# Attention, then a two-layer ELU network, on one core: where v is cast, how reciprocals are spread, and who turns q and k to fp16

## The chip, the cores and the metric

One NeuronCore of a Trainium2 chip runs the whole program in one launch. The time is device time in microseconds (us), from the runs of the program; beside it stands the span of one profiled execution, from its first to its last instruction. Lower is better.

## The reference

```python
B, H, S, D = 8, 8, 576, 64                     # q, k, v: fp32
q_d, k_d, v_d = means of q, k, v over groups of 4 tokens      # 144 tokens
out_d  = softmax(q_d @ k_d.T / 8) @ v_d                       # "global"
scores = where(|i - j| < 4, q @ k.T / 8, -1e9)
local  = softmax(scores) @ v                                  # "local"
x = (repeat(out_d, 4) + local)      # -> 4608 tokens x 512
h = x @ w_in                        # 512 x 2048
g = where(h > 0, h, exp(min(h, 0)) - 1)
out = g @ w_out                     # 2048 x 512, fp32
```

## The kernel before

**Work.** Attention is done by pairs of heads: eight batches b of four pairs j. Local attention runs in six blocks of 96 queries against 102 keys (three more on either side), so v is held as 102 rows. The network is done by nine tiles t of 512 tokens: `mm1(t, fc)` (L561) makes 128 columns of h from four matmuls, takes them through ScalarE (exp, L572) and VectorE (L573, L576); `mm2(t, i)` (L580) is a quarter of an output row block, again four matmuls, and with every fourth ScalarE copies the result (L593) and SyncE stores it (L595).

**One pair.** `early_transposes` (b below 3, L250) or `transposes` (b from 3, L307) turn q and k on TensorE, by products with constants. `flip` (L241, matmul at L244) does it in two halves: head e uses 64 columns of the array and writes 64 partitions. The same step makes the means of v (L273 or L314). ScalarE and VectorE copy the results to `qt`, `kt`, `kd`, `vd`. A memset by VectorE clears the six edge columns of each new `kt` (L259, L327). `scores` (L339) has the products (L346, L361), the exponentials (L369, L375) and the mask (L380). Row sums are made for a batch at a time by `denominators` (L421), with the reciprocal at L448; these 128 x 288 numbers must then be spread over the partitions of the heads. For batch 1 `spread_pe` (L470) does it by matmuls and copies; for batches 2 to 7 `spread_out` and `spread_in` (L451, L456) write them to DRAM and read them back, both from ScalarE's queue. `outputs` (L546) has the last products (L506, L512), two VectorE multiplications (L521, L526) and GpSimd's addition into `xt` (L535), the network's input. Batch 0 has versions of its own, pair by pair (`early_v`, `early_denominators`, `early_spread`, `early_outputs`).

**Loads.** q and k come by half batches n (four heads) through `load_qk` (L194) on GpSimd's queue, which casts to fp16 on the way. v comes by half batches as fp32 through `load_v` (L215) on SyncE's queue: 96 rows, then three rows above and three below. `open_v` (L224) takes the buffers and has GpSimd clear a few elements first, for which SyncE waits. `cast` (L236) turns one pair's v to fp16 on GpSimd. Weights come in eight chunks by `load_weights` (L166) on GpSimd's queue, cast on the way.

**Order.** The schedule is written out by hand. All calls are put in one list of events with a time each and sorted (L663); each engine and each queue works in that order. A unit is about one mm1 and one mm2. The startup is the list `order` with `after`; the network's tile t starts at `start_of(t)`; batch b from 1 on starts at `base` with its pairs at `slots`, its row sums at `d0` and its outputs at `o0`. In `order`, all q and k of batch 0, both halves of v and four weight chunks are issued before the first cast of v. Results of the transposes, scores, outputs and spreads share two PSUM buffers (`two`, L131), so each waits for the copies out of the one before the last.

Of the kernel before, what the change touches and what calls it, by code (L numbers as in the profile page):

```python
# [19 lines left out]
QW = QB + 24  # L20
# [9 lines left out]
NHALF = 2 * B  # L30
# [70 lines left out]
def kernel(  # L101
# [76 lines left out]
    stq, stk, stv, stv32 = {}, {}, {}, {}  # L178
    stT, stB, stS, stR = {}, {}, {}, {}

    def heads(b, j):

        n, a = 2 * b + j // 2, 2 * (j % 2)
        return stq[n], stk[n], stv[n], a

    def blocks(src, n, lo, hi, tok, rows_):

        a = src[n // 2, 4 * (n % 2)]
        return bass.AP(
            tensor=a.tensor, offset=a.offset + (QB * lo + tok) * D,  # L190
            ap=[[D, rows_], [QB * D, hi - lo], [1, D]],
        )

    def load_qk(n, pairs_=(0, 1)):  # L194
        if n not in stq:
            stq[n] = sb.tile([QB, 4, NB, 64], FP16, tag="q16", bufs=3, name="q16")
            stk[n] = sb.tile([QB, 4, NB, 64], FP16, tag="k16", bufs=3, name="k16")
        h0, h1 = 2 * pairs_[0], 2 * pairs_[-1] + 2
        for src, dst in ((q, stq[n]), (k, stk[n])):
            if n < 2 * NRUN:  # L200
                a = src[n // 2, 4 * (n % 2) + h0]
                nc.gpsimd.dma_start(
                    out=dst[:, h0:h1].rearrange("p h c d -> p h (c d)"),
                    in_=bass.AP(
                        tensor=a.tensor, offset=a.offset,
                        ap=[[NB * D, QB], [S * D, h1 - h0], [1, NB * D]],
                    ),
                )
            else:
                nc.gpsimd.dma_start(  # L210
                    out=dst[:].rearrange("p h c d -> p (h c) d"),
                    in_=blocks(src, n, 0, 4 * NB, 0, QB),
                )

    def load_v(n):  # L215
        v32 = stv32[n]
        lo = 1 if n == 0 else 0
        hi = 4 * NB - (1 if n == NHALF - 1 else 0)
        to = v32[:].rearrange("p h c d -> p (h c) d")
        nc.sync.dma_start(out=to[3:99], in_=blocks(v, n, 0, 4 * NB, 0, QB))  # L220
        nc.sync.dma_start(out=to[0:3, lo:], in_=blocks(v, n, lo, 4 * NB, -3, 3))
        nc.sync.dma_start(out=to[99:KW, 0:hi], in_=blocks(v, n, 0, hi, QB, 3))

    def open_v(n):  # L224

        v32 = sb.tile([KW, 4, NB, 64], FP32, tag="v32", bufs=2, name="v32")
        if n == 0:
            nc.gpsimd.memset(v32[0:3, 0, 0, :], 0.0)
        if n == NHALF - 1:
            nc.gpsimd.memset(v32[96:KW, 3, NB - 1, :], 0.0)  # L230
        if n < 2 * NRUN:
            nc.gpsimd.memset(v32[:, 0, 0, 0:1], 0.0)
        stv32[n] = v32
        stv[n] = sb.tile([KW, 4, NB, 64], FP16, tag="v16", bufs=4, name="v16")

    def cast(b, j):  # L236
        n, a = 2 * b + j // 2, 2 * (j % 2)
        nc.gpsimd.tensor_copy(out=stv[n][:, a : a + 2], in_=stv32[n][:, a : a + 2])  # L238
# [11 lines left out]
    def early_transposes(b, j):  # L250
        q16, k16, v16, a = heads(b, j)
# [5 lines left out]
        kt = sb.tile([128, S + 6], FP16, tag="kt", bufs=2, name="kt")  # L257
        kd = sb.tile([128, SD], FP16, tag="kd", bufs=2, name="kd")
        nc.vector.memset(_free(kt[:, 0:1], [[S + 3, 2], [1, 3]]), 0.0)  # L259
        tq, tk = two("tq"), two("tk")  # L260
        for t, x16 in ((tq, q16), (tk, k16)):
# [8 lines left out]
            if b >= NEARLY:  # L270
                g = 0 if t is tq else 1
                for c in range(3):
                    nc.tensor.matmul(  # L273
                        t[0:KG, 0, HB : HB + 128], VR[:, 48 - 24 * c : 120 - 24 * c],
                        v16[:, a : a + 2, 3 * g + c, :], start=(c == 0), stop=(c == 2),
# [14 lines left out]
    def early_v(b, j):  # L290

        mex, dex, _ = stS[(b, j)]
        _, _, v16, a = heads(b, j)
        rb = early_two("rb")
        VR = consts["VR"]
        for c in range(NB):
            nc.tensor.matmul(  # L297
                rb[0:KG, c // 3, 360:488], VR[:, 48 - 24 * (c % 3) : 120 - 24 * (c % 3)],
                v16[:, a : a + 2, c, :], start=(c % 3 == 0), stop=(c % 3 == 2),
# [7 lines left out]
    def transposes(b, j):  # L307
        q16, k16, v16, a = heads(b, j)
        VR, QI = consts["VR"], consts["QI"]
        tq, tk = two("tq"), two("tk")  # L310
        for c in range(NB):
            flip(tq, q16, a, c, (c // 3, QW * (c % 3)), QW, QI, start=True, stop=True)
        for c in range(NB):
            nc.tensor.matmul(  # L314
                tq[0:KG, c // 3, 3 * QW : 3 * QW + 128],
                VR[:, 48 - 24 * (c % 3) : 120 - 24 * (c % 3)], v16[:, a : a + 2, c, :],
# [6 lines left out]
        for c in range(NB):  # L323
            flip(tk, k16, a, c, (c // 3, QW * (c % 3)), QW, QI, start=True, stop=True)
        tk4 = tk[:, :, 0 : 3 * QW].rearrange("p g (c w) -> p g c w", w=QW)
        kt = sb.tile([128, S + 6], FP16, tag="kt", bufs=2, name="kt")
        nc.vector.memset(_free(kt[:, 0:1], [[S + 3, 2], [1, 3]]), 0.0)  # L327
# [173 lines left out]
    def output_products(b, j, lg):  # L501
        mex, dex, vd = stS.pop((b, j))
        _, _, v16, a = heads(b, j)
        for c in range(NB):
            for e in range(2):
                nc.tensor.matmul(  # L506
                    lg[64 * e : 64 * e + 64, c // 3, QB * (c % 3) : QB * (c % 3) + QB],
                    v16[:, a + e, c, :], mex[:, e, QB * c : QB * c + QB], start=True, stop=True,
# [93 lines left out]
    def at(time, fn, *args):  # L602
# [5 lines left out]
        (load_consts, 0, 3), (load_qk, 0, (0,)), (load_qk, 0, (1,)), (open_v, 0), (load_v, 0),  # L608
        (load_qk, 1), (open_v, 1), (load_v, 1),
        *((load_weights, i) for i in range(4)), (cast, 0, 0), (cast, 0, 1),  # L610
        (warm, 9), (early_transposes, 0, 0), (warm, 5), (scores, 0, 0), (load_consts, 3, 4),
        (warm, 5), (load_weights, 4), (load_weights, 5), (cast, 0, 2), (cast, 0, 3),
        (load_weights, 6), (load_weights, 7),
    ]
    after = {2: ((open_v, 2), (load_v, 2), (load_qk, 2)),
             3: ((load_qk, 3), (open_v, 3), (load_v, 3))}
# [11 lines left out]
    def start_of(t):  # L628
        return 0 if t == 0 else 16 * t + (16 if t == 1 else 20)
# [66 lines left out]
```

## Time and profile before

| | |
|---|---|
| runs, median of 3 (least, most) | 417.18 us (414.22, 418.7) |
| the profiled execution's own time | 414.35 us |
| its span | 412.6 us |
| mean granted TensorE clock | 0.953 |
| busy: TensorE, VectorE, ScalarE, GpSimd | 372.1, 253.1, 202.0, 107.4 us |
| first matmul on v of batch 0 (L297) | at 25.41 us |
| first mm1 (L567) | at 46.13 us |
| first transposes of batch 1 | at 58.50 us |
| two blocks of four 512-column matmuls, start to start | 0.87 us |
| VectorE, min with -1 added (L573), mean of 144 | 0.371 us |

How to read it: PE is TensorE, PEld its loads of weights, DVE VectorE, ACT ScalarE, POOL GpSimd, SP SyncE; a q behind a name is that engine's queue, where it issues a DMA. L238 is line 238 of the code. Busy time of PE is taken from modelled ends, so what counts for it is the time from one start to the next. In a line of the timeline stand the start and the length in us, the engine, the line, the operation, the result, what it reads, the shapes, how many were merged, and in brackets the idle time before it with what ended it.

### The profile page before, as it was taken

How to read it: one execution, taken by the hardware profiler on the slowest of the kernel's cores; microseconds unless marked ns; L12 is line 12 of the kernel's file. 1: busy time of each engine (PE TensorE's matmuls, PEld its weight loads, DVE VectorE, ACT ScalarE, POOL GpSimd, SP SyncE). 2: the span in 40 equal slices, each digit the busy share in tenths (PEclk: the TensorE clock that was granted, in tenths of full speed). 3: DMA queues.
4: the chain of work that ended last, by engine and by line, in shares of the span. 5: the costliest groups of instructions: out<-in, count | busy, mean ns of one | idle time of the engine just before them, and what ended most of it. 6: DMA issues, size and time to landing. Idle time of an engine off the chain costs nothing.

```text
span 412.6 us, 9302 instructions
## 1 busy us (share of the span) xinstructions
PE 372.1 (90%) x3847; PEld 191.6 (46%) x3847; DVE 253.1 (61%) x520; ACT 202.0 (49%) x381; POOL 107.4 (26%) x150
## 2 busy tenths in 40 slices
PE   8057898978986899999989999999999899999996
PEld 4045344545543455554545554545545354444442
DVE  2127497465863866686758676866867585555520
ACT  3025256624654466647554756475656334444421
POOL 7025543007430372072307130820230050000000
PEclk9759698999995799999999999999999999999999
DMA  8996979222997099709980999092200401010111
GB/s 142 215 188 100 187 130 193 55 55 36 180 130 115 2 116 96 159 27 149 92 154 29 168 82 169 21 151 53 81 27 25 106 27 51 25 52 26 52 52 76
DMA packets 107993, 39.16 MB, mean 95 GB/s; under 512 B 90540, under 2 KB 103214, under 8 KB 107950
## 3 DMA queue, kind: packets, MB, share of 16 engines
q0 software_dynamic: 55456, 13.63, 34.9%
q1 hardware_dynamic: 44698, 19.47, 21.4%
q10 hardware_dynamic: 7796, 5.46, 5.7%
q8 instruction: 30, 0.49, 0.5%
q14 instruction: 13, 0.11, 0.1%
HBM read 42.30 MB, written 9.88 MB: 126 GB/s over the span
## 4 chain that ended last, share of the span: by engine, by line
PE 72%; DVE 10%; DMA 6%; ACT 5%; ACTq 3%; issue 2%; SPq 1%; POOL 1%; DVEq 0%; POOLq 0%
PE op L587 27%; PE hp L567 26%; DMA v<-in_v_dram 4%; PE sc L346 4%; DVE gt L576 3%; PE tq L244 3%; PE tk L244 3%; ACTq L461 3%; PE lg L506 2%; DMA rd<-rc 2%; PE tq L314 2%; DVE e L573 2%; DVE rc L448 1%; ACT pex L369 1%; ACT e L572 1%
## 5 line engine op out<-in xcount | busy, mean ns | idle before, releaser
L567 PE MATMUL hp<-xt,WI 128*128 128x512 f16 x576 | 151.8, 391 | 7.7 <-DVE gt L576 6.2
L587 PE MATMUL op<-WO,gt 128*128 128x512 f16 x576 | 145.4, 380 | 0.0
L572 ACT ACTIVATE e<-hp 128x512 f16<-128x512 f32 x144 | 85.7, 599 | 102.3 <-PE hp L567 81.5
L576 DVE SCALAR_TENSOR_TENSOR gt<-hp,e 128x512 f16<-128x512 f32 x144 | 99.6, 691 | 5.3
L567 PEld LDWEIGHTS <-WI 128*128 128x128 f16 x576 | 54.7, 100 | 75.3 <-issue 15.9
L573 DVE TENSOR_SCALAR e<-e 128x512 f16<-128x512 f16 x144 | 53.5, 371 | 57.7 <-ACT e L572 56.5
L535 POOL TENSOR_TENSOR xt<-ln,gn 128x512 f16<-128x512 f16 (+7 forms) x64 | 42.6, 694 | 157.7 <-DVE ln L526 157.6
L587 PEld LDWEIGHTS <-gt 128*128 128x128 f16 x576 | 53.5, 98 | 62.8 <-issue 0.5
L369 ACT ACTIVATE pex<-sc 102x576 f16<-102x576 f32 x64 | 41.4, 646 | 36.7 <-PE sc L361 36.4
L238 POOL CAST v<-v 102x768 f16<-102x768 f32 x32 | 26.1, 831 | 67.0 <-DMA v<-in_v_dram 56.9
L380 DVE TENSOR_TENSOR mex<-pex,const 102x1152 f16<-102x1152 f16 x28 | 21.7, 776 | 26.4 <-ACT pex L369 26.0
L593 ACT COPY os<-op 128x512 f32<-128x512 f32 x36 | 21.2, 588 | 17.9 <-PE op L587 17.9
L375 ACT ACTIVATE dex<-sc 72x288 f16<-72x288 f32 x64 | 25.8, 403 | 0.0
L346 PE MATMUL sc<-qt,kt 64*102 64x96 f16 x384 | 18.9, 221 | 4.8 <-DVE kt L284 2.8
L346 PEld LDWEIGHTS <-kt 64*102 64x102 f16 x384 | 13.5, 129 | 19.6 <-ACT e L572 6.3
L244 PEld LDWEIGHTS <-q 96*64 96x64 f16 x528 | 14.5, 111 | 15.7 <-issue 14.3
L244 PE MATMUL tq<-const,q 96*64 96x96 f16 (+1 forms) x528 | 19.0, 215 | 2.3 <-DVE ln L526 1.3
L526 DVE TENSOR_TENSOR ln<-lg,rcb 128x576 f16<-128x576 f32 x28 | 20.9, 746 | 0.0
L320 ACT CAST qt<-tq 128x720 f16<-128x720 f32 x20 | 15.1, 757 | 10.0 <-PE tq L314 10.0
L328 ACT CAST kt<-tk 128x576 f16<-128x576 f32 x20 | 12.8, 641 | 14.3 <-DVE kt L327 12.0
L244 PE MATMUL tk<-const,k 96*64 96x96 f16 (+1 forms) x528 | 18.9, 215 | 0.1
L297 PE MATMUL rb<-v,const 102*72 102x128 f16 x24 | 2.4, 244 | 15.6 <-POOL v L238 14.4
(67 smaller groups left out, 269.1 us busy)
## 6 DMA issues: line engine op xcount, KB each, us to landing
v<-in_v_dram SPq DMA_DIRECT2D x16, 576.0 KB
out_dram<-os SPq DMA_DIRECT2D x36, 256.0 KB
q<-in_q_dram POOLq DMA_DIRECT2D x15, 288.0 KB, 7.5
k<-in_k_dram POOLq DMA_DIRECT2D x15, 288.0 KB, 8.9
rcb<-rd ACTq DMA_DIRECT2D x12, 288.0 KB
WI<-in_moe_w_in_dram POOLq DMA_DIRECT2D x4, 512.0 KB, 17.0
WO<-in_moe_w_out_dram POOLq DMA_DIRECT2D x4, 512.0 KB, 7.6
rcb<-rd ACTq DMA_DIRECT2D x12, 72.0 KB
```

The lines of the kernel that those rows point to most:

```text
L238: nc.gpsimd.tensor_copy(out=stv[n][:, a : a + 2], in_=stv32[n][:, a : a + 2])
L244: nc.tensor.matmul(t[64 * e : 64 * e + 64, col[0], col[1] : col[1] + w] if len(col) == 2 else col[2](t[64 * e : 64 * e + 64, 1, col[1] : c ...
L346: nc.tensor.matmul(sc[e][0:KW, c // 3, QB * (c % 3) : QB * (c % 3) + QB], kt[r, QB * c : QB * c + KW], qt[r, QB * c : QB * c + QB] if run ...
L369: nc.scalar.activation(out=pex[:, e, :].rearrange("p (g u) -> p g u", g=2), in_=sc[e][0:KW, :, 0:HB], func=AF.Exp, scale=SCALE,)
L375: nc.scalar.activation(out=dex[:, e], in_=sc[e][0:KG, :, HB : HB + SD], func=AF.Exp, scale=SCALE,)
L380: nc.vector.tensor_tensor(out=mex[:], in0=pex[:], in1=mk2, op=AB.mult)
L535: nc.gpsimd.tensor_tensor(out=xt(t)[:, j, t0 - TBLK * t : t1 - TBLK * t], in0=ln[:, a:z], in1=_rep4(gn[:, a // 4 : z // 4]), op=AB.add,)
L567: nc.tensor.matmul(hp[:], WI[:, dc, 128 * fc : 128 * fc + 128], x[:, dc, :], start=(dc == 0), stop=(dc == DMC - 1),)
L572: nc.scalar.activation(out=e[:], in_=hp[:], func=AF.Exp)
L573: nc.vector.tensor_scalar(out=e[:], in0=e[:], scalar1=1.0, scalar2=-1.0, op0=AB.min, op1=AB.add)
L576: nc.vector.scalar_tensor_tensor(out=gts[t][:, fc, :], in0=hp[:], scalar=0.0, op0=AB.max, in1=e[:], op1=AB.add)
L587: nc.tensor.matmul(op_[:], gts[t][:, fc, 128 * tt : 128 * tt + 128], WO[:, fc, :], start=(fc == 0), stop=(fc == FCN - 1),)
```

## The change

**v and its cast.** v is loaded pair by pair (`load`), three SyncE loads each, into buffers of one pair (three of them). In the startup the first pair's v is issued after the first pair's q and k; weight chunk 0 comes after the cast of pair 0, chunk 1 after that of pair 2, chunks 2 and 3 after that of pair 3, chunks 4 to 7 after the outputs of pairs 0 and 1. v as fp16 is laid out by block, then head.

**Reciprocals.** Batch 2, too, is spread by `spread_pe`.

**Batches 3 to 7.** q and k are loaded pair by pair as fp32 on SyncE's queue, and `cast` turns q, k and v to fp16 on GpSimd, with the two heads of a block side by side. `transposes` then flips both heads with one matmul over the whole array.

**Beside these.** `kt` has two fixed buffers, cleared once. Batch 1 starts at 15.5 instead of 11.5, with closer pairs; tiles from 1 on start 3 units later; mm2 of tile 0 comes every 1.35 units instead of 1.5; batch 2's outputs come 1.5 to 1.7 units sooner after its start.

```diff
+    kts = [sb.tile([128, S + 6], FP16, tag=f"kt{i}", bufs=1, name=f"kt{i}") for i in range(2)]
+    for t in kts:
+        nc.vector.memset(_free(t[:, 0:1], [[S + 3, 2], [1, 3]]), 0.0)
...
+    def load(b, j):
...
+        ts = []
+        if b >= NRUN:
+            for src, name in ((q, "q32"), (k, "k32")):
+                t = sb.tile([QB, 2, NB, 64], FP32, tag=name, bufs=3, name=name)
+                nc.sync.dma_start(out=flat(t), in_=rows(src, 0, 2 * NB, 0, QB))
+                ts.append(t)
+        v32 = sb.tile([KW, 2, NB, 64], FP32, tag="v32", bufs=3, name="v32")
+        lo, hi = 0, 2 * NB
+        if (b, j) == (0, 0):
+            lo = 1
+            nc.gpsimd.memset(v32[0:3, 0, 0, :], 0.0)
+            nc.gpsimd.memset(v32[:, 0, 1, 0:1], 0.0)
...
+        nc.sync.dma_start(out=to[3:99], in_=rows(v, 0, 2 * NB, 0, QB))
+        nc.sync.dma_start(out=to[0:3, lo:], in_=rows(v, lo, 2 * NB, -3, 3))
+        nc.sync.dma_start(out=to[99:KW, 0:hi], in_=rows(v, 0, hi, QB, 3))
+        st32[(b, j)] = (*ts, v32)
+
     def cast(b, j):
-        n, a = 2 * b + j // 2, 2 * (j % 2)
-        nc.gpsimd.tensor_copy(out=stv[n][:, a : a + 2], in_=stv32[n][:, a : a + 2])
+        st16[(b, j)] = []
+        for t, name in zip(st32.pop((b, j)), ("q16", "k16", "v16") if b >= NRUN else ("v16",)):
+            p = t.shape[0]
+            if name == "v16":
+                x = sb.tile([p, NB, 2, 64], FP16, tag=name, bufs=8, name=name)
+            else:
+                x = sb.tile([p, 2, NB, 2, 64], FP16, tag=name, bufs=3, name=name)[:, 0]
+            nc.gpsimd.tensor_copy(
+                out=x if name != "v16" else x[:], in_=t[:].rearrange("p e c d -> p c e d")
+            )
+            st16[(b, j)].append(x)
...
     def transposes(b, j):
...
         for c in range(NB):
-            flip(tq, q16, a, c, (c // 3, QW * (c % 3)), QW, QI, start=True, stop=True)
+            nc.tensor.matmul(
+                tq[:, c // 3, QW * (c % 3) : QW * (c % 3) + QW], q16[:, c], QI, start=True, stop=True
+            )
...
     order = [
-        (load_consts, 0, 3), (load_qk, 0, (0,)), (load_qk, 0, (1,)), (open_v, 0), (load_v, 0),
-        (load_qk, 1), (open_v, 1), (load_v, 1),
-        *((load_weights, i) for i in range(4)), (cast, 0, 0), (cast, 0, 1),
-        (warm, 9), (early_transposes, 0, 0), (warm, 5), (scores, 0, 0), (load_consts, 3, 4),
-        (warm, 5), (load_weights, 4), (load_weights, 5), (cast, 0, 2), (cast, 0, 3),
-        (load_weights, 6), (load_weights, 7),
+        (load_consts, 0, 3), (load_qk, 0, (0,)), (load, 0, 0), (load_qk, 0, (1,)), (load_qk, 1),
+        (load, 0, 1), (load, 0, 2), (cast, 0, 0), (load_weights, 0), (load, 0, 3), (cast, 0, 1),
+        (load, 1, 0), (warm, 9), (early_transposes, 0, 0), (warm, 5), (scores, 0, 0),
+        (load_consts, 3, 4), (warm, 5), (cast, 0, 2), (load, 1, 1), (load_weights, 1), (cast, 0, 3),
+        (load, 1, 2), (load_weights, 2), (load_weights, 3),
     ]
-    after = {2: ((open_v, 2), (load_v, 2), (load_qk, 2)),
-             3: ((load_qk, 3), (open_v, 3), (load_v, 3))}
+    after = {0: ((load_weights, 4), (load_weights, 5)), 1: ((load_weights, 6), (load_weights, 7)),
+             2: ((load_qk, 2),), 3: ((load_qk, 3),)}
...
-        return 0 if t == 0 else 16 * t + (16 if t == 1 else 20)
+        return 0 if t == 0 else 16 * t + (19 if t == 1 else 23)
...
-            base, slots, d0, o0 = 11.5, (0, 1.4, 3.1, 4.5, 6.2, 7.6, 9.3, 10.7), 12.0, (17.2, 18.4)
+            base, slots, d0, o0 = 15.5, (0, 1.4, 2.8, 4.2, 5.6, 7.0, 8.4, 9.8), 12.0, (17.2, 18.4)
...
-            base, slots, d0, o0 = start_of(b) - 24, TIGHT, 12.8, (20.4, 22)
+            base, slots, d0, o0 = start_of(b) - 24, TIGHT, 12.8, (18.9, 20.3)
...
-            n = 2 * b + j // 2
+            n = NPAIR * b + j + 3
             at(base + (slots[2 * j - 2] if j else -3.1) + 0.1, cast, b, j)
+            if n < len(pairs):
+                at(base + slots[2 * j] + 0.2, load, *pairs[n])
+            if b + 1 < NRUN and j % 2:
+                at(base + slots[2 * j] + 0.3, load_qk, 2 * b + 2 + j // 2)
...
-        if b == 1:
+        if b < NRUN:
             at(base + d0 + 2.4, spread_pe, b, 0)
             at(base + d0 + 3.3, spread_pe, b, 2)
...
-            at(16 + 1.5 * s + 0.75 if t == 0 else start_of(t + 1) + s + 0.75, mm2, t, s)
+            at(16 + 1.35 * s + 0.75 if t == 0 else start_of(t + 1) + s + 0.75, mm2, t, s)
```

## The prediction

> **What bounds the kernel now.** I read the busy slices first, for where TensorE (PE) is short of work; then the waits and the chain, for what it waits for; then the timeline of those places; last one stretch where PE is full.
>
> ```profile
> PE   8057898978986899999989999999999899999996
> PEclk9759698999995799999999999999999999999999
> ```
>
> A slice is 10.3 us. There are two holes: near 11 to 25 us, and around 120 to 135 us, each with a lowered clock. From slice 14 on PE is full. So the first 145 us are bounded by waits and the rest by PE's own instructions.
>
> ```profile
> PE rb L297 <- POOL v L238: 14.4, 1, 14.4
> POOL v L238 <- DMA v<-in_v_dram: 56.9, 8, 16.0
> ```
> ```profile
> 8.48 15.90 DMA v<-in_v_dram
> ```
>
> The waits (us in total, times, longest) and the chain agree: PE stands 14.4 us for the cast of the first v, and that for a load of v that ends at 24.38. The packets in the trace say why: v's begin at 6.0 us and run at about 400 per us until 10, then, once the 1024-byte packets of the weights run beside them, at 55 to 160 per us.
>
> ```profile
> 119.08 1.95 DVE L448 RECIPROCAL rc<-den 128x288 f16<-128x288 f32 x1
> ...
> 127.86 2.65 ACTq L461 DMA_DIRECT2D rcb<-rd  x4
> 130.55 0.60 ACT L572 ACTIVATE e<-hp 128x512 f16<-128x512 f32 x1 [4.75 <-issue]
> 132.25 1.87 PE L567 MATMUL hp<-xt,WI 128*128 128x512 f16 x4 [3.08 <-DVE gt L576]
> ```
>
> The second hole (timeline: start, us, instruction): batch 2's reciprocals go through DRAM, ScalarE (ACT) stands 4.75 us in that, the first mm1's exponentials stand behind it, and PE waits 3.08 us.
>
> ```profile
> 165.81 0.51 PE L244 MATMUL tq<-const,q 96*64 96x120 f16 x12
> 166.24 0.53 PE L314 MATMUL tq<-v,const 102*72 102x128 f16 x6
> 166.70 0.51 PE L244 MATMUL tk<-const,k 96*64 96x120 f16 x12
> 167.14 1.04 PE L587 MATMUL op<-WO,gt 128*128 128x512 f16 x4
> 168.01 1.03 PE L567 MATMUL hp<-xt,WI 128*128 128x512 f16 x4
> ```
>
> PE in the full part: 0.87 us from one block of four 512-column matmuls to the next, 0.44 us for 12 half-array flips. (T(b,j) below: the transposes of pair j of batch b; block: four matmuls of mm1 or mm2.)
>
> **The change part by part.** The profiled execution took 414.35 us (span 412.6); the runs' median, 417.18, is 2.8 above it. The sum is against 414.35.
>
> *1. Startup.* v comes by pairs, three SyncE (SP) loads each; v(0,0) goes ahead of most of q and k, and its memset now stands behind two of POOL's DMA issues (1.31 to 2.73), not four, so SP issues at about 3.2, packets from 4.9 (1.7 us later, as in the trace). It needs 1152 packets and two small ones instead of 2304. Beside it run the 1190 or so q/k packets left, at 145 per us (6 to 12 us): 8.2 us, so v(0,0) lands at about 13.5. Bounds: 8 us at 390 packets per us (then PE's own end of T(0,1) at 11.4 counts) and 24.4 as now. I take 13.5, with rows for both queues behind it. Cast 0.83: PE resumes at about 15, not 25.4. Batch 0 then takes the 20.7 us of 25.41 to 46.13: mm1 begins at 35.7. POOL's weight issues (0.76 each) now wait for casts: chunk 0 at 15, chunk 1 at 19, 2 and 3 at about 24, the rest behind batch 0's sums of xt, which wait for DVE's ln. At 155 packets per us (16 to 24 us) the 4096 weight packets and at 190 batch 1's 768 first q/k packets take 30.5 us from about 17, with 2 us of gap: 50. mm1 of tile 0, now all 16 blocks before T(1,0), takes 16 x 0.9 and 1.7 for the low clock: 51.8. So T(1,0) stands at 51.8 against 58.50, with 16 blocks done instead of 12 (3.5 us): **-10.2**, bounds 0 and -13.
>
> *2. Batch 1.* T(1,0) to T(1,2) took 13.5 us (58.50 to 72.04) with five blocks between. With mm2 alone between, T(1,2) to T(1,3) took 4.82 (72.04 to 76.86), so 9.6 with four blocks: 3.9 less, less one block of 0.87: **-3.0**. Into batch 2 mm1 stands one block closer to the xt that it needs (0.9), and each of four pairs has a block fewer around it (0.5 each): **+3**. Bounds of both: -5 and +5, the idle around the same steps now.
>
> *3. Batch 2's reciprocals by PE.* Added, by batch 1's rows: 12 matmuls (0.48 and 0.67 us), four casts each on ACT and DVE (0.64 and 0.28; 0.76 and 0.30, twice). Removed: five ACT DMAs (0.33, 2.65) and the 4.75 us. New waits: both PSUM pairs are held by the scores' exponentials (2.1 us on ACT) when the first spread comes, with no block between; the second and the next transposes wait for casts (0.55 and 1.05); the outputs come right after scores (2.0). Queued behind each on PE are the blocks of mm1. From the end of den I get 22.5 us to T(3,2), where now 25.4 go by (118.15 to 143.58); DVE is then nearly full: **-2** after taking out the part of step 4 in it. Bounds: +3 if the clock falls twice, -5 if it never does (it is 0.5 from 124.7 to 138.3).
>
> *4. Whole-array flips, batches 3 to 7.* Starts of the single matmuls: two halves go side by side every 53 ns, so six whole flips of 120 columns cost no less than twelve halves: 0.32 us. What goes is the switching. From flips to L314 it is 146 ns instead of 53, L314 to flips 149 instead of 56, block to flips 309 instead of 216, flips to block 148 instead of 53; within each run the first step is 74 instead of 53. Between 128*128 forms, and from 102*72 (L273) to 128*128, there is no such gap (55 to 56 ns). 93+93+93+95+21+21 = 416 ns a pair; two of the 20 pairs are in step 3: 18 x 0.416 = **-7.5**. Bounds 0 (the 96-row weights switch too) and -8.3. I take the full gain: L412's whole-array matmuls follow each other every 42 ns.
>
> The Trainium skill (TensorE: Matmul & The Clock Gate, Part 3) has small matmuls in different column tiles run concurrently; the trace agrees (4 ns between two halves). It names no cost of changing tiles; by it alone step 4 would be 0 and the sum 7.5 us higher.
>
> *5. Casts on GpSimd (POOL).* Added: 40 casts of 96x768 at 0.83 by L238, 33 us. Removed: 20 DMA issues of 1.18, 23.6 us. The stretch now:
>
> ```profile
> L238 POOL CAST v<-v 102x768 f16<-102x768 f32 x32 | 26.1, 831 | 67.0 <-DMA v<-in_v_dram 56.9
> ```
> ```profile
> 225.53 1.19 POOL L210 DMA_DIRECT2D q<-in_q_dram  x1
> 225.81 1.01 DVE L573 TENSOR_SCALAR e<-e 128x512 f16<-128x512 f16 x1 [0.19 <-ACT e L572]
> ```
>
> DVE's 0.29 us operation took 1.01, ending where POOL's ended. 28 of the 144 are stretched so, 11.5 us for 107 us of POOL; 10 us more make about **+1**, bounds 0 and +3. Per batch POOL then has 12 x 0.83 + 5.3 (sums of xt) = 15.3 of 38 us, and each cast stands some 7 us ahead of its transposes. That is the cover; without it a pair would wait 2.5 us.
>
> The Trainium skill (SBUF — State Buffer, Who interferes with whom) makes the port that DVE's fast modes share with GpSimd an exclusive lock, the loser waiting the whole instruction. This speaks against the change and the row agrees. If by it every new cast held one DVE operation for its length, my estimate is 33 us of DVE over five batches, which DVE's idle quarter would hide.
>
> *6. Queues, at nothing.* SP gets 40 loads of q and k and 48 more of v, some 0.35 us each to issue: about 7 us in 38; its stores wait 260 us for ACT anyway, and os has three buffers (without that cover a store would stand behind L221's 1.3 to 5.8 us). The 46,080 packets of q and k double to 256 bytes and take about 22 ns (v's) instead of 32, so the DMA engines get less to do. Loads run three pairs ahead. The memsets of kt (0.06) go; ACT's 12 us behind them are off PE's chain where PE is full.
>
> Sum: -10.2 - 3.0 + 3 - 2 - 7.5 + 1 = -18.7: 395.7, so **396**.
>
> **The rivals.** *A: the startup gains nothing.* v(0,0) comes as late as now, or batch 1's q and k do, because the weight chunks stand behind casts on POOL. For it: a DMA share of 0.78 to 1.16 over the first 72 us. Against it: q0 idles for some 6 us now (34 to 39, 26 to 28). 396 + 10 = 406.
>
> *B: the flips gain nothing*, since 96-row weights cost the same switch: 396 + 7.5 = 403.5. Against it: L273 to L567 without a gap at 102 rows.
>
> *C: no gain but the flips'.* Steps 1 to 3 come to 0 (A, and batch 2 with two clock drops): 414.35 - 7.5 + 1 = 408; with B as well 415, no difference.
>
> *D: slower.* The casts read 64-element runs in another order than they write; if one takes t us, a batch needs 12t + 5.3 on POOL. At t = 2.7 POOL equals the 38 us of a batch, and the change is slower from t = 3.1. At 3.4 it is 46 against 38: 8 x 5 = 40 more, 436. Against it: the slowest row, two inputs and a repeated operand (L535, 512 elements in 1.09), gives 1.6 us for 768.
>
> **How the numbers follow.** Forecast 0.60, A 0.15, B 0.10, C 0.08 (0.02 of it at 408, the rest with B near 415), D 0.07. The likeliest's own range is 386 to 404 (bounds of 1, 2 and 3 added half-way). To 410 it takes in A, B and C at 408; left out are D, the rest of C and a tail below 386. About 1% (4 us) is what a measurement can tell from no change, so faster means under 413: forecast, A, B and 0.02 of C, 0.87; same 0.06; slower 0.07.
>
> **What would show it.** Step 1: first L297 near 15 us, first L567 near 36, T(1,0) near 52. Step 2: about 4.8 us between batch 1's transposes. Step 3: no L461 before batch 3's, PE waits under 2.5 us around it, and the clock. Step 4: flips, L314 and flips in about 1.0 us instead of 1.33, a pair's cost 0.4 less. Step 5: POOL casts near 0.8 us, no PE wait for them. I am wrong if PE waits for POOL's casts in the full part, if the weights hold mm1, or if switches stay.

## The result, and the profile after

The changed kernel takes 397.14 us (median of 4 runs, 395.13 to 398.75) against 417.52 for the kernel before in the same series (4 runs, 414.22 to 418.7): ratio 0.952, 95% interval 0.945 to 0.959. Medians and ranges are of all runs of a series; each ratio with its interval leaves out runs more than 1.5% above the fastest of the same kernel. In a later series (c_after, below) the same code took 400.08 (395.23 to 403.77, 6 runs), ratio 0.960, interval 0.953 to 0.967. Forecast were 396 and "faster"; both medians lie in the range. The profiled execution took 396.7 us, span 394.9, mean clock 0.970.

The slices of the page after (9.9 us each):

```profile
PE   8777999779777799999999999999999899999995
PEclk9995999998986999999999999999999999999999
```

In slices 1 to 3, where PE had 0, 5 and 7, it now has 7, 7 and 7; slices 10 to 13, those of batch 2 and its reciprocals, stand at 7, with a lowered clock in slices 11 and 12. The places that the prediction named, as stages; T(b,j) is the first flip of pair j of batch b, and behind the stroke stands how many blocks of the network PE has done by then:

| | before | after | change, a block counted as 0.87 | forecast |
|---|---|---|---|---|
| first matmul on v | 25.4 us | 11.8 us | | 15 |
| first mm1 | 46.1 us | 31.7 us | | 35.7 |
| T(1,0) | 58.50 / 12 | 50.14 / 16 | -8.4 - 3.5 = -11.9 | -10.2 |
| T(1,0) to T(2,0) | 30.4, 12 blocks | 27.0, 11 blocks | -3.4 + 0.9 = -2.6 | -3.0 |
| T(2,0) to T(3,0) | 30.2, 16 blocks | 32.4, 13 blocks | +2.2 + 2.6 = +4.8 | +3 |
| T(3,0) to T(4,0) | 38.3 | 38.8 | +0.5 | -2 and -0.8 of step 4 |
| T(4,0) to PE's end | 251.4 | 242.5 | -8.8 | -6.7 and +1 |

The last column sums to -18.7, the one before it to -18.0. The sum was hit; four of its five terms were missed by 1.7 to 3.3 us, two each way.

The startup, timeline of GpSimd and then of PE:

```profile
10.93 0.82 POOL L240 CAST v<-v 102x768 f16<-102x768 f32 x1 [5.53 <-DMA v<-in_v_dram]
11.69 0.75 POOL L174 DMA_DIRECT2D WI<-in_moe_w_in_dram  x1
16.29 0.83 POOL L240 CAST v<-v 102x768 f16<-102x768 f32 x1 [3.84 <-DMA v<-in_v_dram]
```
```profile
11.80 0.49 PE L302 MATMUL rb<-v,const 102*72 102x128 f16 x6 [0.91 <-POOL v L240]
...
15.31 0.50 PE L420 MATMUL rb<-rce,const 128*128 128x96 f16 x8 [1.45 <-DMA const<-const3c]
...
31.70 0.59 PE L575 MATMUL hp<-xt,WI 128*128 128x512 f16 x1 [1.26 <-DVE ln L534]
```

The wait of 14.4 us for the cast of v is down to 0.91, and another wait stands behind it: the fourth constant, the selectors of batch 0's spread, issued behind the first scores.

The full part, one pair (compare the five lines of the prediction):

```profile
156.31 0.48 PE L317 MATMUL tq<-const,q 96*128 96x120 f16 x6
156.63 0.50 PE L321 MATMUL tq<-v,const 102*72 102x128 f16 x6
156.97 0.48 PE L331 MATMUL tk<-const,k 96*128 96x120 f16 x6
157.28 1.03 PE L595 MATMUL op<-WO,gt 128*128 128x512 f16 x4
```

From the first flip to the next block it is 0.97 us where it was 1.33. And batch 2's spread by TensorE:

```profile
114.26 0.28 PE L488 MATMUL rb<-rc,const 32*128 32x288 f16 x1 [1.09 <-ACT dex L383]
...
115.09 0.75 PE L488 MATMUL rb<-rc,const 32*128 32x288 f16 x5 [0.56 <-ACT dex L383]
...
115.78 1.89 PE L575 MATMUL hp<-xt,WI 128*128 128x512 f16 x4
...
117.60 0.78 PE L488 MATMUL rb<-rc,const 32*128 32x288 f16 x6
119.28 0.76 PE L317 MATMUL tq<-const,q 96*128 96x120 f16 x6 [0.90 <-ACT rcb L497]
...
121.08 3.62 PE L575 MATMUL hp<-xt,WI 128*128 128x512 f16 x8
```

Three short waits, 2.55 us, and a block that takes 1.89 us: the clock has gone to half. The windows of the trace (start and end, length, busy times with counts, clock, DMA share, GB/s) put that at 10 us:

```profile
115.00:125.20 10.20, 9.20 (x55) 4.49 (x56) 5.09 (x11) 4.65 (x10) 0.00 (x0) 0.50 0.72 118
```

GpSimd's casts, in the groups of the page:

```profile
L581 DVE TENSOR_SCALAR e<-e 128x512 f16<-128x512 f16 x144 | 56.9, 395 | 55.9 <-ACT e L580 54.3
...
L240 POOL CAST v<-v 102x768 f16<-102x768 f32 x32 | 27.5, 864 | 93.8 <-DMA v<-in_v_dram 93.8
...
L240 POOL CAST q<-q 96x768 f16<-96x768 f32 x20 | 16.8, 839 | 9.4 <-PE tq L278 8.6
L240 POOL CAST k<-k 96x768 f16<-96x768 f32 x20 | 19.1, 954 | 0.9 <-DMA k<-in_k_dram 0.9
```

q's casts take 0.84 us, k's 0.95, and PE waits for none of them in the full part.

### The profile page after: what moved, and what is told of

It reads as the page before. It is cut to its first block, busy times and chain, and to the rows that moved or that the text cites. A ratio compares the mean times of both kernels' runs of the same rounds, so it can differ in the third digit from the quotient of the medians.

```text
span 394.9 us, 9066 instructions
## 1 busy us (share of the span) xinstructions
PE 364.4 (92%) x3619; PEld 191.3 (48%) x3619; DVE 258.4 (65%) x494; ACT 202.7 (51%) x385; POOL 118.5 (30%) x165
## 3 DMA queue, kind: packets, MB, share of 16 engines
q1 hardware_dynamic: 91770, 31.27, 37.1%
## 4 chain that ended last, share of the span: by engine, by line
PE 66%; DVE 12%; ACT 6%; DMA 5%; POOL 4%; ACTq 3%; issue 2%; SPq 1%; POOLq 0%; DVEq 0%
PE op L595 26%; PE hp L575 25%; DVE gt L584 5%; DMA v<-in_v_dram 4%; PE sc L354 3%; ACTq L469 3%; DVE e L581 3%; POOL xt L543 2%; ACT pex L377 2%; ACT e L580 2%; PE lg L514 2%; ACT dex L383 1%; PE tq L321 1%; PE tq L317 1%; PE tk L331 1%
## 5 line engine op out<-in xcount | busy, mean ns | idle before, releaser
L581 DVE TENSOR_SCALAR e<-e 128x512 f16<-128x512 f16 x144 | 56.9, 395 | 55.9 <-ACT e L580 54.3
L240 POOL CAST v<-v 102x768 f16<-102x768 f32 x32 | 27.5, 864 | 93.8 <-DMA v<-in_v_dram 93.8
L388 DVE TENSOR_TENSOR mex<-pex,const 102x1152 f16<-102x1152 f16 x28 | 23.3, 831 | 32.6 <-ACT pex L377 32.6
L354 PE MATMUL sc<-qt,kt 64*102 64x96 f16 x384 | 17.9, 216 | 4.7 <-DVE kt L289 1.7
L534 DVE TENSOR_TENSOR ln<-lg,rcb 128x576 f16<-128x576 f32 x28 | 20.9, 746 | 0.0
L240 POOL CAST q<-q 96x768 f16<-96x768 f32 x20 | 16.8, 839 | 9.4 <-PE tq L278 8.6
L240 POOL CAST k<-k 96x768 f16<-96x768 f32 x20 | 19.1, 954 | 0.9 <-DMA k<-in_k_dram 0.9
L514 PE MATMUL lg<-mex,v 102*64 102x96 f16 x384 | 13.9, 210 | 3.1 <-ACT dex L383 2.7
L286 ACT CAST qt<-tq 128x576 f16<-128x576 f32 x12 | 7.7, 638 | 16.8 <-DVE vd L282 13.4
L514 PEld LDWEIGHTS <-v 102*64 102x64 f16 x384 | 10.9, 110 | 9.2 <-issue 4.8
```

What stands on the lines that cost most here:

```text
L240: nc.gpsimd.tensor_copy(out=x if name != "v16" else x[:], in_=t[:].rearrange("p e c d -> p c e d"))
L354: nc.tensor.matmul(sc[e][0:KW, c // 3, QB * (c % 3) : QB * (c % 3) + QB], kt[r, QB * c : QB * c + KW], qt[r, QB * c : QB * c + QB] if run ...
L388: nc.vector.tensor_tensor(out=mex[:], in0=pex[:], in1=mk2, op=AB.mult)
L514: nc.tensor.matmul(lg[64 * e : 64 * e + 64, c // 3, QB * (c % 3) : QB * (c % 3) + QB], v16[:, c, e, :], mex[:, e, QB * c : QB * c + QB], s ...
L581: nc.vector.tensor_scalar(out=e[:], in0=e[:], scalar1=1.0, scalar2=-1.0, op0=AB.min, op1=AB.add)
```

## The experiments

Eleven runs. All of them compute the whole output. My theory was the list of terms of the prediction; the rivals were that each of them is worth nothing, or comes from another part of the change. Since the change is made of parts that touch each other, they were tried in pairs, so that each part is seen with the old and with the new of its partner.

### Flips and loads: e1_halves and b2_whole

*e1_halves*: the changed kernel with the flips of batches 3 to 7 in two halves again (q's are shown, k's alike).

```diff
-            nc.tensor.matmul(
-                tq[:, c // 3, QW * (c % 3) : QW * (c % 3) + QW], q16[:, c], QI, start=True, stop=True
-            )
+            for e in range(2):
+                nc.tensor.matmul(
+                    tq[64 * e : 64 * e + 64, c // 3, QW * (c % 3) : QW * (c % 3) + QW],
+                    q16[:, c, e, :], QI, start=True, stop=True,
+                )
```

> The changed kernel with one part undone: batches 3 to 7 flip q and k in two halves again (12 matmuls over 64 columns each instead of 6 over 128); loads, casts on GpSimd, order and buffers stay. Theory (TensorE pays about 93 ns at each switch between 64-column and whole-array steps, four switches and two slow first steps a pair, 0.416 us): T(4,0) to the last matmul, 242.55 us in the changed kernel, grows by 16 x 0.416 = 6.7 us, the whole by 7.5 to 8.3, to about 405 us. Rival (halves run side by side, so the form is free, and what batches 3 to 7 gained came from the loads): no growth, 397 us.

404.14 us (402.13 to 408.85), ratio 0.967 (0.959 to 0.975). The profiled execution took 408.85 us; from batch 4 on its clock is 1.00, and only that part of it is read here. From T(4,0) to PE's end it takes 249.5 us against 242.5, 7.0 more where the theory had 6.7. The same pair as above, with half flips:

```profile
161.86 0.51 PE L318 MATMUL tq<-const,q 96*64 96x120 f16 x12
162.30 0.53 PE L323 MATMUL tq<-v,const 102*72 102x128 f16 x6
162.75 0.51 PE L334 MATMUL tk<-const,k 96*64 96x120 f16 x12
163.19 1.04 PE L599 MATMUL op<-WO,gt 128*128 128x512 f16 x4
```

From the first flip to the block it is 1.33 us again. The starts of the single matmuls in the two traces (medians of 15 pairs) put the difference at the switches: from a block to the flips 309 ns with halves and 216 after, from q's flips to the means of v 146 and 52, from these to k's flips 149 and 56, from there to the next block 148 and 52. (Where the row sums follow the flips, once in four pairs, the last step stays at 146 ns in both.)

*b2_whole*: the other way round, the kernel before with whole-array flips but no casts of q and k on GpSimd: its casting loads write the two heads of a block side by side, head by head.

```diff
-                nc.gpsimd.dma_start(
-                    out=dst[:].rearrange("p h c d -> p (h c) d"),
-                    in_=blocks(src, n, 0, 4 * NB, 0, QB),
-                )
+                for h in range(4):
+                    a = src[n // 2, 4 * (n % 2) + h]
+                    nc.gpsimd.dma_start(
+                        out=by_block(dst)[:, h // 2, :, h % 2],
+                        in_=bass.AP(
+                            tensor=a.tensor, offset=a.offset, ap=[[D, QB], [QB * D, NB], [1, D]],
+                        ),
+                    )
```

> The kernel before with one part of the change alone, made in another way: q and k of batches 3 to 7 are still cast by the DMA, but one DMA for each head writes them with the two heads of a block side by side (eight issues on GpSimd's queue for two before), and the flips take the whole array. No casts on GpSimd. Theory (the switches): T(4,0) to the last matmul, 251.4 us before, falls by 6.7 us, the whole by 7.5 to 8.3, to about 409 us, if GpSimd's six more issues for a half batch (some 0.7 us each) stay beside other work. Rival (the gain in batches 3 to 7 is that loads moved from GpSimd's queue to SyncE's, with fewer packets and less hold on VectorE): no gain or a loss, 417 us or more.

412.26 us (411.26 to 414.05), ratio 0.988 (0.981 to 0.995), between the theory's 409 and the rival's 417: T(4,0) to PE's end falls by 2.0 us, not by 6.7.

With the two kernels of the change these make a square. The windows from T(4,0) to T(7,3), 15 pairs, of the kernel before, of e1_halves, of b2_whole and of the kernel after (the length, then PE's busy time):

```profile
157.50:309.80 152.30, 149.90 (x1579) 76.81 (x1578) 108.55 (x219) 89.03 (x166) 43.26 (x56) 1.00 0.72 96
```
```profile
153.50:304.10 150.60, 149.03 (x1581) 76.58 (x1582) 110.02 (x204) 88.91 (x166) 55.36 (x73) 1.00 0.61 129
```
```profile
156.40:307.10 150.70, 145.81 (x1400) 77.11 (x1399) 107.62 (x219) 88.48 (x166) 63.05 (x90) 0.99 0.72 97
```
```profile
148.30:292.30 144.00, 143.14 (x1400) 76.47 (x1399) 111.70 (x204) 88.45 (x166) 55.73 (x73) 1.00 0.64 135
```

| length, and PE not busy in it | half flips | whole flips |
|---|---|---|
| q and k cast in the load | 152.3, 2.4 | 150.7, 4.9 |
| q and k cast by GpSimd | 150.6, 1.6 | 144.0, 0.9 |

With the new loads the flips are worth 6.6 us of 15 pairs, 0.44 each; forecast were 0.416, all of it from the switching. Rival B falls. With the old loads the switches go too (the same starts as after: 216, 52, 56 and 52 ns) and PE's instructions shrink by 4.1 us, but its gaps grow by 2.5: b2_whole issues more on GpSimd, and batch 5's hole, where the reciprocals go through DRAM, is longer there (T(5,1) to T(5,2) 18.74 us against 17.23 before and 15.64 after), with the clock at half for 3.4 us in it. So in these four kernels the flips' gain arrives in full only with the new loads and their casts, and these cost nothing by themselves: 152.3 to 150.6. Forecast was a loss of 1 for the casts. Loads and casts were not tried apart, nor a way to load two heads side by side with fewer issues. Why PE's busy time falls by 4.1 us in one row and by 5.9 in the other isn't settled; its ends are modelled.

### Startup: e3_weights_first and b1_order

*e3_weights_first*: the changed kernel with the four weight chunks of mm1 issued ahead of the first cast.

```diff
-        (load, 0, 1), (load, 0, 2), (cast, 0, 0), (load_weights, 0), (load, 0, 3), (cast, 0, 1),
+        (load, 0, 1), (load, 0, 2), *((load_weights, i) for i in range(4)),
+        (cast, 0, 0), (load, 0, 3), (cast, 0, 1),
...
-        (load_consts, 3, 4), (warm, 5), (cast, 0, 2), (load, 1, 1), (load_weights, 1), (cast, 0, 3),
-        (load, 1, 2), (load_weights, 2), (load_weights, 3),
+        (load_consts, 3, 4), (warm, 5), (cast, 0, 2), (load, 1, 1), (cast, 0, 3), (load, 1, 2),
```

> The changed kernel with the order of the startup changed in one point: weight chunks 0 to 3 are issued before the first cast of v, as before the change; v by pairs and its place stay. Theory (v's packets run slowly beside the weights'): the first pair's v was there before weights could have been, so the first matmul on v stays near 12 us, but v of pairs 1 to 3 comes later and batch 0's later pairs wait: first mm1 from 31.7 to about 36 to 40, while the weights come some 6 us sooner, so T(1,0) moves less; the whole 397 to 403 us. Rival (what counts is v by pairs and its place ahead of q and k; the order of the weights is nothing): first mm1 within 1 us of 31.7 and the whole within 2 us of 397.

403.45 us (402.72 to 408.12), ratio 0.969 (0.961 to 0.978). GpSimd's timeline:

```profile
10.54 1.05 POOL L240 CAST v<-v 102x768 f16<-102x768 f32 x1 [2.12 <-DMA v<-in_v_dram]
19.98 0.83 POOL L240 CAST v<-v 102x768 f16<-102x768 f32 x1 [8.39 <-DMA v<-in_v_dram]
28.13 0.83 POOL L240 CAST v<-v 102x768 f16<-102x768 f32 x1 [7.32 <-DMA v<-in_v_dram]
30.08 0.83 POOL L240 CAST v<-v 102x768 f16<-102x768 f32 x1 [1.12 <-DMA v<-in_v_dram]
```

The first cast is where it was; the second comes 3.7 us later than in the changed kernel and the third 7.6 (20.52 there), each waiting for its load. mm1 starts at 40.6 us, just beyond the 36 to 40 expected, and T(1,0) comes at 57.05: they are 5.8 and 5.4 us later than on the mean of five executions with the unchanged startup (34.8 and 51.6), so T(1,0) did not move less, as the theory had it. So where the chunks are issued matters by what they take from v's transfers, not by GpSimd's time to issue them.

*b1_order*: the kernel before with only the startup's order changed; v still comes four heads at a time.

```diff
-        (load_consts, 0, 3), (load_qk, 0, (0,)), (load_qk, 0, (1,)), (open_v, 0), (load_v, 0),
+        (load_consts, 0, 3), (load_qk, 0, (0,)), (open_v, 0), (load_v, 0), (load_qk, 0, (1,)),
...
-        *((load_weights, i) for i in range(4)), (cast, 0, 0), (cast, 0, 1),
+        (cast, 0, 0), (load_weights, 0), (cast, 0, 1), *((load_weights, i) for i in range(1, 4)),
```

> The kernel before with only the order of the startup's issues changed: the first load of v ahead of the second part of q and k, and the weight chunks 0 to 3 issued after the first cast of v (0), and after the second (1 to 3), where the kernel before issues all four ahead of the casts. The tiles of v stay as they are, four heads to a load. Theory: the first matmul on v starts at 25.4 us in the kernel before since GpSimd sits in the issues of the weight chunks and the load of v lies behind other loads; with the order alone it starts at 12 to 16 us, and the first matmul of the expert layer at 33 to 38 us in place of 46.1. Since batches 1 and 2 keep their slots, 8 to 10 us of it reach the first flip of batch 1 or the end: about 407 to 411 us. Rival: the smaller loads of v (two heads) are what lets v come early; then the first matmul on v stays above 19 us and the time above 412 us.

409.96 us (405.74 to 413.36), ratio 0.983 (0.974 to 0.992). The first cast starts at 17.62 us:

```profile
17.62 0.82 POOL L238 CAST v<-v 102x768 f16<-102x768 f32 x1 [11.95 <-DMA v<-in_v_dram]
```

The first matmul on v follows at 18.5 and mm1 at 39.8: both later than the theory had them and earlier than the rival; the time is the theory's (407 to 411). The order alone takes 6.9 us off the first matmul on v; the other 6.7 (to 11.8) come with the half-sized first load, the main difference that is left up to there. mm1 is at 46.1 before, 39.8 with the order alone, 40.6 with the small loads but the weights ahead of the casts (e3), 31.7 to 36.2 with the startup of the changed kernel.

### The next wait of the startup: e5_const3 and e6_const3mid

mm1 starts at 31.7 us in the profiled execution after, but at 34.8 to 36.2 in the four others with the same startup (e1_halves, e2_dram2, c_after, c_dram2). There PE waits longer for the fourth constant (3.3, 3.2, 2.6 and 1.7 us instead of 1.4), and the half clock falls into batch 0, for 10.2 us from 14.4 to 15.9 on. The slices of the clock in c_after, beside those above:

```profile
PEclk9776999989997999999999999999999999999999
```

Two kernels, made from e2_dram2 (below), issue it earlier.

```diff
-        (load_consts, 0, 3), (load_qk, 0, (0,)), (load, 0, 0), (load_qk, 0, (1,)), (load_qk, 1),
+        (load_consts, 0, 4), (load_qk, 0, (0,)), (load, 0, 0), (load_qk, 0, (1,)), (load_qk, 1),
...
-        (load_consts, 3, 4), (warm, 5), (cast, 0, 2), (load, 1, 1), (load_weights, 1), (cast, 0, 3),
+        (warm, 5), (cast, 0, 2), (load, 1, 1), (load_weights, 1), (cast, 0, 3),
```

> The changed kernel with batch 2 spread through DRAM, and one more edit: the fourth constant (352 KB, the selectors with which batch 0 spreads its reciprocals) is issued on the queue of ScalarE right behind the first three, at about 2 us in place of 8.2 us. In the kernel without that edit the first spread of batch 0 waits for it until 16.2 us, some 3.3 us, and the clock then falls to half for 10 us. Theory: this wait ends last in the startup; without it the first expert matmul starts at about 30 to 32 us in place of 35.3, and 2 to 4 us reach the end: about 391 to 393 us against 394.9. Rival: 352 KB more ahead of the first q, k and v delay those by 1.5 to 2 us (about 176 GB/s go there), which moves the same wait to the first flips and the first matmul on v; then the time stays at 394 to 397 us.

393.3 us (392.7 to 394.45), ratio 0.948 (0.940 to 0.955). *e6_const3mid* issues it between the first flips and the first scores:

```diff
-        (load, 1, 0), (warm, 9), (early_transposes, 0, 0), (warm, 5), (scores, 0, 0),
-        (load_consts, 3, 4), (warm, 5), (cast, 0, 2),
+        (load, 1, 0), (warm, 9), (early_transposes, 0, 0), (warm, 5), (load_consts, 3, 4), (scores, 0, 0),
+        (warm, 5), (cast, 0, 2),
```

> As the last, but the fourth constant is issued between the first flips and the first scores of batch 0, behind ScalarE's copies of the flips (at about 6.5 us in place of 8.2 us). Theory: some 1.7 us of the wait of 3.3 us go, and the first q, k and v, which have landed or are on their way by then, aren't delayed: about 393 us. Rival: the wait is set by the queue's bandwidth, shared with the loads of v and of q and k at that time, and not by the issue; then the fourth constant lands within 0.5 us of 16.2 us as before and the time stays at 394 to 396 us.

393.4 us (391.18 to 397.33; the profiled execution took 397.33), ratio 0.945 (0.937 to 0.953). PE's longest waits in the first 50 us, of e5_const3 and of e6_const3mid:

```profile
PE tk L249 <- DMA k<-in_k_dram: 2.0, 1, 2.0
```
```profile
PE rb L302 <- POOL v L240: 5.1, 1, 5.1
```

The wait for the constant is gone in both. In its place PE waits 2.0 us for k in e5_const3 and 5.1 us for v in e6_const3mid, and its first matmul on v starts at 15.3 and 16.2 us instead of 10.9 (e2_dram2). mm1 is at 35.4 and 36.9. The mechanism of e5's rival holds, the wait moved (by 2.2 us to k in c_const3, too); the time, 393.3, lies between the two texts. e6's time is its theory's, but its trace doesn't bear the theory out: the constant came in time, and the first v was cast at 15.3 us instead of 10.0. Whether the constant delayed it isn't shown; this is one execution, and the other three took 391.2 to 394.1 us. That the transfers of the first 16 us are the limit, and not the place of one of them, fits e5_const3 and c_const3; it was not tried with fewer bytes.

### Reciprocals of batch 2: e2_dram2 and b3_pe2

*e2_dram2*: the changed kernel with batch 2 sent through DRAM, as before.

```diff
-        if b < NRUN:
+        if b == 1:
             at(base + d0 + 2.4, spread_pe, b, 0)
```

> The changed kernel with one part undone: batch 2's reciprocals go through DRAM again. Theory after the result (the stall of ScalarE behind DRAM was replaced by waits of TensorE for two PSUM pairs and by a clock at 0.5 from 115.0 to 125.2, so this part gave nothing): T(3,0) to T(4,0), 38.84 us in the changed kernel, within 2 us of that, and the whole within 3 us of 397. Rival (the part is worth its hole, some 5 to 9 us, and something else took that back): 402 to 406 us.

394.89 us (392.98 to 398.98), ratio 0.945 (0.936 to 0.953). T(3,0) to T(4,0) takes 33.4 us against 38.8. Both the theory (no difference there) and the rival (402 to 406 us) were wrong: this part of the change loses 5.4 us there. The timeline shows what takes its place, in this execution with the clock at full speed:

```profile
113.65 0.33 ACTq L461 DMA_DIRECT2D rd<-rc  x1
...
115.25 0.65 ACTq L469 DMA_DIRECT2D rcb<-rd  x1
...
119.65 1.02 PE L575 MATMUL hp<-xt,WI 128*128 128x512 f16 x4 [1.61 <-DVE gt L584]
```

The first mm1 waits 1.61 us instead of 3.08. ScalarE, which stood 4.75 us in the detour before, now issues the reading back between exponentials. The chains of waits of the kernel before and of e2_dram2 have the store of the reciprocals (start, length; in the first view batch 2's, then batch 4's, in the second batch 2's):

```profile
122.39 5.39 DMA rd<-rc
...
202.66 3.40 DMA rd<-rc
```
```profile
113.65 1.58 DMA rd<-rc
```

and the DMA queues in those two stretches (packets, MB, share of the 16 engines' time) show what ran beside it:

```profile
q0 software_dynamic: 2320, 0.29, 91.5%
q1 hardware_dynamic: 1326, 0.33, 39.9%
q10 hardware_dynamic: 144, 0.07, 4.4%
```
```profile
q10 hardware_dynamic: 144, 0.07, 14.0%
```

q10 carries the same 144 packets in both. Before, GpSimd's casting loads (q0) and v's (q1) ran beside them; in the kernel with the new loads nothing does. The kernel before shows the same from batch to batch. From the issue of the store to that of the reading back it takes 5.5 us in batch 2; 3.4 and 2.4 in batches 4 and 5, where q0's packets run beside it; 1.7, 1.6 and 2.1 in batches 3, 6 and 7, where none do. In all thirteen traces eleven such stores had packets of q0 beside them and took 2.2 to 6.0 us; 62 had none of q0 or q1 and took 1.6 to 2.1, but for two (3.4 and 3.6 us, in c_dram2 and e1_halves), so something else can lengthen it too. If the loads beside the store are what makes the detour dear, then TensorE's spread should be neither gain nor loss in the kernel before. *b3_pe2* is the kernel before with that one edit:

```diff
-        if b == 1:
+        if b < NRUN:
             at(base + d0 + 2.4, spread_pe, b, 0)
```

> The kernel before with one edit: the reciprocals of batch 2 are spread by TensorE, as those of batch 1 are, and everything else stays. With the new loads the part lost 5.4 us of the stretch from the first flip of batch 3 to the first flip of batch 4 (38.8 us with TensorE, 33.4 us through DRAM); the kernel before has 38.3 us there with the detour through DRAM. Theory: the detour was dear in the kernel before only because two queues of loads ran beside its store (5.39 us to land, 1.6 us without them), so that taking it away gives about what the spread by TensorE costs: the stretch stays at 38 to 40 us and the whole time within 2 us of 417.5. Rival: the spread by TensorE is cheap in itself, and what makes it dear in the changed kernel is its place beside the new loads and casts; then the stretch falls by 4 to 5 us, to about 34 us, and the time to about 413 us.

418.75 us (415.0 to 421.89, 10 runs), ratio 1.004 (0.999 to 1.009); T(3,0) to T(4,0) 39.7 us against 38.3. The theory holds: with TensorE's spread this stretch takes 36.6 to 39.7 us with either loads (after, c_after, e3_weights_first, b3_pe2; 40.4 in e1_halves, with half flips), the detour 38.3 to 39.2 with the old ones (before, b1_order, b2_whole) and 32.5 to 34.3 with the new (five executions). Cut at T(3,1), the same traces show the two sides of the exchange:

| T(3,0) to T(3,1), T(3,1) to T(3,2), us | spread by TensorE | through DRAM |
|---|---|---|
| old loads (b3_pe2, before) | 10.95, 14.88 | 5.91, 18.56 |
| new loads (after, e2_dram2) | 9.80, 15.31 | 4.31, 15.78 |
| new loads, second series (c_after, c_dram2) | 9.50, 14.23 | 4.31, 16.38 |

The spread costs 5.0 to 5.5 us in the first part, whichever loads run. What it removes in the second part is 3.7 us with the old loads and 0.5 to 2.2 with the new. The clock is in these numbers: between T(3,0) and T(4,0) it falls to half in all five executions with the spread and all three with the old loads and the detour, but in two of five with the new loads and the detour; one of the two is c_dram2, with the same 33.4 us as e2_dram2. That the old loads, and not the other places that batch 2's outputs and the blocks have in the changed kernel, made the hole is argued from the stores; the schedule alone wasn't tried.

### The versions side by side: c_after, c_dram2, c_const3

> The changed kernel itself, unedited, beside the two versions below on one chip: 395 to 399 us, with the stretch from the first flip of batch 3 to the first flip of batch 4 at 38 to 40 us again. If that stretch comes out below 36 us here, the loss put down to the spread of batch 2 by TensorE was an accident of one execution.

> The changed kernel with batch 2 spread through DRAM, unedited otherwise, beside the changed kernel on one chip. Theory: the spread by TensorE loses 5 us of the stretch from the first flip of batch 3 to the first flip of batch 4, and the stretch is 33 to 34 us here; of the time 2 to 5 us are gained, since the startup varies by as much from one execution to the next: 392 to 396 us. Rival: what the stretch gains is lost again by the end; then the two are within 1 us.

> As the last, with the fourth constant at 2 us. Its one execution so far started the expert layer no earlier (35.4 us against 35.3), but ran at a granted clock of 0.991 in place of 0.972. Theory: the wait only moved, so it's within 1 us of the last. Rival: without the wait at 13 us the half clock of the startup stays away in most executions, and it is 2 to 3 us below the last with a narrower spread of times.

c_after is the kernel after, c_dram2 that of e2_dram2, c_const3 that of e5_const3, on one chip: 400.08 (395.23 to 403.77), 395.35 (393.79 to 397.92) and 395.3 us (390.94 to 397.79), 6 runs each; ratios 0.960 (0.953 to 0.967), 0.953 (0.946 to 0.959) and 0.949 (0.942 to 0.956). The stretch from T(3,0) to T(4,0): 37.1, 33.4 and 32.5 us. c_after missed its text on both counts, by 1 us each, but stays above the 36 us from which the loss would have been an accident; c_dram2 came out as its theory had it. Batch 2 through DRAM is 4.7 us better here and was 2.3 better in the first results (394.89 against 397.14, not one series); the intervals overlap, the stretch does not. That is the best version found. The earlier constant adds nothing that can be measured: 395.3 against 395.35, as its theory said.

## Why the prediction was right, and where it was not

*1. Startup, right in kind.* v(0,0) was cast at 10.93 us instead of 13.5 and mm1 came at 31.7 in one execution, at 34.8 to 36.2 in four others, where 35.7 stood. Over five executions with the unchanged startup (50.1, 52.7, 51.7, 52.4, 51.2) T(1,0) is at 51.6, so this term is -10.4 on their mean and -11.9 in the profiled one; -10.2 was forecast. b1 and e3 show both halves of the mechanism. Rival A falls. Not forecast was the wait behind it, the fourth constant; issuing it earlier moved the wait and gained nothing.

*2. Batch 1, right; into batch 2, too low.* -2.6 against -3.0, T(1,1) to T(1,2) and on 4.8 us each as forecast. Into batch 2 the loss was +4.8, not +3. A term that the sum doesn't have lies there: the clock was at half for 3.4 us from 87.65 on, and in the kernel before it wasn't in this stretch. In c_const3, without such a fall, the stretch took 30.8 us instead of 32.4, +3.2 by the same count; but c_after took 30.9 with one, so it isn't settled.

*3. Batch 2's reciprocals, wrong in sign.* The step "From the end of den I get 22.5 us to T(3,2)", where 25.4 went by before, failed: it took 25.9 (108.68 to 134.60), and 24.5 and 24.1 in c_after and e3_weights_first. What was mis-sized is the cost of what was added. The waits for exponentials and casts came to 2.55 us, about as listed. The bounds spoke of two falls of the clock and of none; one came, and to the next start the block at 115.78 took 1.82 us instead of 0.87, the flips at 119.28 1.80 instead of 0.97, two blocks at 121.08 3.54 (the scores follow at 124.62) instead of 1.74: 3.6 us, as much as the miss of 3.4. How much of a fall the 22.5 held isn't said, and no run has the spread without one. The price of what was removed, 25.4 us, is a measured one and not where the sum failed; but it was no price of the detour alone. With the new loads, another part of the same change, the detour takes 20.9 us over the same stretch (110.75 to 131.64 in e2_dram2), and this part of the change loses: 5.4 us from T(3,0) to T(4,0) against e2, 1.4 in the kernel before by b3.

*4. Whole-array flips, right.* 0.44 a pair with the new loads against 0.416, by e1, and the single starts show it at the switches. Rival B falls by e1, C by the startup's gain. The sum has a slip here: step 3 takes the flips of two pairs out of its 2.9 us, and step 4 leaves the same two out of its 20, so that 0.8 us are counted nowhere; with them it would be -19.5, 395. (The range, too, isn't quite what it says: half of the bounds of steps 1 to 3 gives about 390 to 406 instead of 386 to 404. Both medians lie in either.)

*5. Casts on GpSimd, right that they hide; the +1 doesn't show.* It was taken for VectorE's operations held up behind GpSimd's. The row agrees that there are more of them (L581 0.395 us instead of 0.371, 3.4 us over 144), but nothing on PE's path shows it: from before to e1, both with half flips, the stretch got 1.7 us shorter; the new loads and the casts can't be told apart in that, so whether the casts alone cost 1 us stays open. Rival D falls: 0.84 to 0.95 us a cast is far from the 3.1 from which it decides.

*6. Queues, at nothing: right for SyncE, incomplete otherwise.* That q and k leave GpSimd's queue was counted as less work for the DMA engines; that it clears the way for the DRAM detours of batches 4 and 5 wasn't. Their stores took 3.4 and 2.4 us before and 1.7 each after, and T(5,1) to T(5,2), where batch 4's detour lies, went from 17.23 to 15.64 us, and to 15.30 in e1_halves with half flips.

So 396 came out right with the mechanisms of steps 1, 2 and 4 right. That it came out within 1.2 us is luck: step 3 (3.3 us too good) and the way into batch 2 (1.8) were offset by the startup (1.7 the other way, in this execution) and by 4 to 6 together (-8.8 against -5.7).

## What to carry to other kernels

Price a wait by what runs beside it, not only by the instruction that it is filed under: when one part of a change removes a neighbour (here, casting loads beside a small DRAM store), another part's gain can vanish or turn into a loss, so each part has to be costed against the kernel with the other parts in. In the full part of a kernel bound by TensorE, count the starts where matmuls of different array halves follow each other; a layout that lets small steps use the whole array can pay for extra casts on an idle engine. In a startup full of transfers, moving one of them forward can just move the wait to another, as it did here. And a sum that is hit is no proof of its terms: here four of five were off.

## What the runs showed of the hardware

- Going between matmuls on half the array's columns and whole-array ones costs time at each switch: the step from one form to the other took 146 to 149 ns where steps between whole-array forms took 52 to 56, and 309 where it took 216; 6.6 us over 15 pairs with four switches and two runs of halves each.
- A 72 KB store to DRAM took 1.58 us with its queue alone and 5.39 us with two queues of loads beside it, for the same 144 packets. Of 62 such stores without these loads two took 3.4 and 3.6 us to the reading back, for no reason that was found.
- Around the short gaps of batch 2's spread (1.09, 0.56 and 0.90 us) the granted clock was 0.50 for 10.2 us, in which a block took 1.89 us instead of 1.03. After one gap of 1.61 us in the same place it stayed at full speed in e2_dram2; in c_dram2, the same kernel with the same gap, it fell for 6.8 us from 123.96 on. There the fall lay where PE waits for VectorE in e2_dram2, and the stretch took 33.4 us in both. One startup put its first stretch of half clock, 10.2 us, at 14.4 to 15.9 us in four executions and at 29.6 in another.
